# Feed-forward input tiles in pairs of d_ff halves, difference halves made early, scores and values at later slots, ninth chunks of two batches per transfer

## The chip, the cores and the metric

The program runs on one core of one Trainium2 chip. The metric is the device time of one execution in microseconds. The kernel before was run three times: 289.43 us is the median, 286.65 and 290.04 us the lowest and the highest.

## The reference

The inputs are `q`, `k`, `v` of shape 8 batches x 8 heads x 576 positions x 64, and the two weights `w_in` (512 x 2048) and `w_out` (2048 x 512), all float32. Attention stays inside chunks of 64 positions, so each batch has nine chunks per head:

```python
scores = scale * np.matmul(q_c, k_c.transpose(0, 1, 2, 4, 3))     # chunk by chunk
attn = softmax(scores)
x = attn @ v_c            # -> 4608 tokens x 512 (heads side by side)
h = np.maximum(x @ w_in, 0.0)
out = (h * h) @ w_out     # 4608 x 512
```

## The kernel before

**Tiling.** The 4608 tokens are cut into 18 groups of 256 tokens (four chunks of 64), and two groups make a block of 512 tokens: blocks j = 0 to 8. Sixteen groups ("whole") hold four chunks that follow each other in one batch. A batch has nine chunks, so the ninth chunks of all batches are left over; they make groups 14 and 15 (`rest`, line 47), that is block 7. `chunks` gives the four (batch, position) pairs of a group.

**Stages of a block.** For its two groups: load q and k (lines 99 to 121) and v (`v_pieces`, 145 to 153); cast q and k to bf16 (`C`, `cast_qk`, on ScalarE for groups 8 and up); transpose them by DMA (`TD`, line 267); scores and exponential (`SC`, `scores`: 32 small matmuls per group at line 290 and one Exp at 301); values (`AV`, `values`: 32 matmuls at 317 in two tiles, each of which VectorE evicts with a reciprocal at 324 and a multiplication at 325); a DMA transpose of the result x into xT (`XT`, line 338). Then the feed-forward input stage `ffn_in` and the output stage `ffn_out` of the block.

**`ffn_in(j)`** (line 375) makes 16 tiles of d_ff, `ft` = 0 to 15. Each is four matmuls of 128x512 (line 380) into one of four PSUM banks `ps_ffn`, a Relu on ScalarE into `rl` (391), and a square into `gT[:, ft]`: on VectorE (395), or on ScalarE (393) for the `ft` in `SQUARES_ON_ACT`. In blocks 2 to 8 the order is `FT_ORDER`, 8 to 15 and then 0 to 7.

**`ffn_out(j)`** (line 413) multiplies the 512 x 2048 gT by the 2048 x 512 w_out with seven products of quarters in place of eight (Strassen's scheme in Winograd's form). The quarters of gT are a11, a12 (first 256 tokens, `ft` 0 to 7 and 8 to 15) and a21, a22 (last 256 tokens). Each product is 16 matmuls of 128x256 (line 448), 8 for each of two row tiles. The products follow each other as n = a22(b11+b21); m = a11(b12+b22); n += d5 b22; m += d2 b11; n += d1(b11-b22); m += d6(b11+b12); n += d7(b21+b22), in two PSUM banks called n and m. Between them a bank is read out: n1 and n2 by ScalarE copies (492, 501), `nm` (496) and the outputs c21, c12, c22 (508, 517, 522) by VectorE additions, and c11 by a ScalarE copy (528). The next product into a bank waits for that reading. The differences d5 = a11-a12, d2 = a22-a21, d1 = a11-a22, d6, d7 are made by VectorE at line 408, each one instruction on 128x2048 bf16 elements, all inside `ffn_out`: d5 and d2 at its start, d1 after `nm`, d6 after n2, d7 after c21.

**Order of the work.** It is written out by hand. Every `yield` of `ffn_in` (16, slots 0 to 15) and of `ffn_out` (14, slots 16 to 29, one for each half product) is a slot; the loop at line 610 puts the attention of the next block (`nxt`), and the casts and transposes of the block after that (`far`), behind chosen slots of block j. Engines take their instructions in the order in which they stand. In the kernel before, the slots are (lines 642 to 661): scores of both groups at 5, 6, 7 or 8, by block; values at 8 and 12, 9 and 13, or 10 and 14; XT three slots behind each; C at 18 and 22; TD at 20 and 24. Block 2 has its own: scores 8 and 10, values 12 and 15.

**SyncE's queue** issues all loads and all DMA transposes of these blocks. `go_slots` says behind which slots one load each is put: every slot from 0 on, but in block 3 slots 0 to 5 and 13 to 31. A load waits for no other engine here, so it is issued as soon as the queue reaches it and one of eight DMA semaphores is free (each DMA waits for the one that stands eight places before it to have landed). A whole group has 3 loads of q and k and 4 or 5 of v; a `rest` group has 8 and 8, since each chunk is from another batch (`runs`, line 89). Outputs are issued from GpSimd's queue (lines 471 and 476).

Of the kernel before, what the change touches and what calls it, by code (L numbers as in the profile page):

```python
# [10 lines left out]
FP32 = mybir.dt.float32  # L11
# [6 lines left out]
def kernel(  # L18
# [22 lines left out]
    blocks = [[g, g + 1] for g in range(0, n_grp, 2)]  # L41


    CH = GT // 4
    n_ch = S // CH
    whole = [[(b, CH * (4 * i + c)) for c in range(4)] for b in range(B) for i in range(2)]
    rest = [[(b, CH * (n_ch - 1)) for b in range(b0, b0 + 4)] for b0 in range(0, B, 4)]
    chunks = whole[:-2] + rest + whole[-2:]

    def is_whole(g):  # L50
# [27 lines left out]
    NV = 5  # L78
    NO = 2 * NV + 1
    v_even = [w_pool.tile([128, 2, n_hp, D + 1], FP32, name=f"ve_sb{i}") for i in range(NV)]  # L80
    v_odd = [w_pool.tile([128, n_hp, D + 1], FP32, name=f"vo_sb{i}") for i in range(NO)]
    for vt in v_even:
        nc.gpsimd.memset(vt[:, :, :, D:D + 1], 1.0)
    for vt in v_odd:
        nc.gpsimd.memset(vt[:, :, D:D + 1], 1.0)

    qk = {}

    def runs(g):

        for t in range(2):
            (b, s), (b1, s1) = chunks[g][2 * t:2 * t + 2]
            if b == b1:
                yield t, 0, 2 * CH, b, s
            else:
                yield t, 0, CH, b, s
                yield t, CH, CH, b1, s1

    def qk_pieces(g):
        q_sb = in_pool.tile([128, 2, H, D], FP32, name="q_sb")  # L100
        k_sb = in_pool.tile([128, 2, H, D], FP32, name="k_sb")
        qk[g] = (q_sb, k_sb)

        def pairs(dst, src, p, m, b, s):
            return lambda: nc.sync.dma_start(
                out=dst.rearrange("p t h d -> p (t h d)")[p:p + m // 2, :].rearrange(
                    "p (h e) -> p h e", h=H),
                in_=src[b, :, s:s + m, :].rearrange("h (s i) d -> s h (i d)", i=2))

        if is_whole(g):  # L110
            yield pairs(q_sb, q, 0, GT, *chunks[g][0])
        else:
            for c in range(4):
                yield pairs(q_sb, q, c * CH // 2, CH, *chunks[g][c])
        if g < FIRST_DMA_T:
            yield pairs(k_sb, k, 0, GT, *chunks[g][0])
            return
        for t, p, m, b, s in runs(g):
            yield lambda t=t, p=p, m=m, b=b, s=s: nc.sync.dma_start(
                out=k_sb[p:p + m, t, :, :],  # L120
                in_=k[b, :, s:s + m, :].rearrange("h s d -> s h d"))

# [2 lines left out]
    for g in range(n_grp):  # L127
        if is_whole(g):
            if g % 2 == 0:
                first = n_odd  # L130
                n_odd += 5
            b, s = chunks[g][0]
            for c in range(4):
                odd_tile[g, c] = first + g % 2 * 2 + (c + 1) // 2
            odd_loads[g] = [(first, CH, CH, b, s), (first + 1, 0, 2 * CH, b, s + CH),
                            (first + 2, 0, 2 * CH, b, s + 3 * CH)] if g % 2 == 0 else [
                                (first + 3, 0, 2 * CH, b, s + CH), (first + 4, 0, CH, b, s + 3 * CH)]
        else:
            for c in range(4):
                odd_tile[g, c] = n_odd + c // 2  # L140
            odd_loads[g] = [(n_odd + c // 2, (1 - c % 2) * CH, CH, b, s)
                            for c, (b, s) in enumerate(chunks[g])]
            n_odd += 2

    def v_pieces(g):
        for t, p, m, b, s in runs(g):
            yield lambda t=t, p=p, m=m, b=b, s=s: nc.sync.dma_start(
                out=v_even[g % NV][p:p + m, t, :, 0:D],
                in_=v[b, 0::2, s:s + m, :].rearrange("h s d -> s h d"))
        for n, p, m, b, s in odd_loads[g]:  # L150
            yield lambda n=n, p=p, m=m, b=b, s=s: nc.sync.dma_start(
                out=v_odd[n % NO][p:p + m, :, 0:D],
                in_=v[b, 1::2, s:s + m, :].rearrange("h s d -> s h d"))

    def go(pieces):
# [147 lines left out]
    def values(g, tiles=(0, 1)):  # L303
        e = state["e", g]
        veb = v_even[g % NV].bitcast(BF16)
        vob = [v_odd[odd_tile[g, c] % NO].bitcast(BF16) for c in range(4)]
        if 0 in tiles:
            state["x", g] = att_pool.tile([128, 2, n_hp, 2, D], BF16, name="x", bufs=3)
        x = state["x", g]
# [58 lines left out]
            transpose_x_early(g, t)  # L368

    gTs = {}  # L370
    FT_ORDER = [*range(n_ft // 2, n_ft), *range(n_ft // 2)]

    def ffn_in(j, parts):
        if j not in gTs:
            gTs[j] = ffn_pool.tile([128, n_ft, BT], BF16, name="gT")
        gT, xT = gTs[j], xTs[j]
        for u, (c, n, ft) in enumerate((c, n, ft) for c, n, fts in parts for ft in fts):
            h = ps_ffn.tile([128, 512], FP32, name="ps_ffn")
            for dt in range(n_dt):
                nc.tensor.matmul(  # L380
                    out=h[:, 0:n],
                    lhsT=w_in_bf[:, dt, ft * 128:(ft + 1) * 128],
                    rhs=xT[:, c // 128:(c + n) // 128, dt, :],
                    start=(dt == 0), stop=(dt == n_dt - 1))
# [6 lines left out]
            nc.scalar.activation(out=rl[:, 0:n], in_=h[:, 0:n], func=AF.Relu)  # L391
            if (n == 512 and ft in SQUARES_ON_ACT) or (n < 512 and (j == 0 or ft in (12, 3))):
                nc.scalar.activation(out=gT[:, ft, c:c + n], in_=rl[:, 0:n], func=AF.Square)  # L393
            else:
                nc.vector.tensor_tensor(  # L395
                    out=gT[:, ft, c:c + n], in0=rl[:, 0:n], in1=rl[:, 0:n], op=ALU.mult)
            yield

    HF, HD = n_ft // 2, d_model // 2
    b11, b12 = w_out_bf[:, 0:HF, 0:HD], w_out_bf[:, 0:HF, HD:]
    b21, b22 = w_out_bf[:, HF:, 0:HD], w_out_bf[:, HF:, HD:]
    b11_p_b21, b11_m_b22, b11_p_b12 = (w_sum[:, i] for i in range(3))
# [8 lines left out]
    def ffn_out(j):  # L413
# [2 lines left out]

        gT = gTs.pop(j)
        HT = BT // 2  # L420
        last = j == len(blocks) - 1
        a11, a12 = gT[:, 0:HF, 0:HT], gT[:, HF:, 0:HT]
        a21, a22 = gT[:, 0:HF, HT:], gT[:, HF:, HT:]

        def difference(x, y):
            d = wst_pool.tile([128, 1024], FP32, name="w_st").bitcast(BF16).rearrange(
                "p (a f) -> p a f", a=HF)
            add(nc.vector, d, x, y, ALU.subtract)
            return d
# [34 lines left out]
        def store(dma, o_sb, half, col, t):  # L464
# [3 lines left out]
            if not is_whole(g):  # L468

                for p in range(2):  # L470
                    dma.dma_start(
                        out=out.rearrange("(b s) d -> s b d", s=S)[
                            s0:s0 + CH, b + p:b + 4:2, col:col + HD],
                        in_=o_sb[p * CH:(p + 1) * CH].rearrange("p (t d) -> p t d", d=HD))
            elif t is None:
                dma.dma_start(  # L476
# [7 lines left out]
        def o_tile():  # L484
            return ffn_pool.tile([128, n_tt * HD], FP32, name="o_sb", bufs=4)

        d5 = difference(a11, a12)
        d2 = difference(a22, a21)
        yield from product("n", a22, b11_p_b21, True)
        n1 = kept("n1")  # L490
        for ps, cols, t in parts("n"):
# [2 lines left out]
        w = kept("nm")  # L494
        for ps, cols, t in parts("m"):
            add(nc.vector, w[:, cols], ps, n1[:, cols])
        d1 = difference(a11, a22)
        yield from product("n", d5, b22, False)
        n2 = kept("n2")
        for ps, cols, t in parts("n"):  # L500
            nc.scalar.copy(out=n2[:, cols], in_=ps)  # L501
        d6 = difference(a21, a11)
        if j == 1:
            d7 = difference(a12, a22)
        yield from product("m", d2, b11, False)
        c21 = o_tile()
        for ps, cols, t in parts("m"):
            add(nc.vector, c21[:, cols], w[:, cols], ps, ALU.subtract)
            store(nc.gpsimd, c21, 1, 0, t)
        if j > 1:  # L510
            d7 = difference(a12, a22)
        yield from product("n", d1, b11_m_b22, False)
        s = kept("n1")
        for ps, cols, t in parts("n"):
# [50 lines left out]
            yield from v_pieces(g)  # L565


    HT = BT // 2
    first_ffn_in = ffn_in(0, [(0, HT, (0, 1)), (HT, HT, (0, 1)), (0, BT, range(2, n_ft))])

    go(pieces([0, 1]))
# [38 lines left out]
    for j, grps in enumerate(blocks):  # L610
# [29 lines left out]
            at(20, sum_quarters(b21_p_b22, b21, b22), None)  # L640
            phases = [ffn_in(1, [(0, 256, FT_ORDER), (256, 256, FT_ORDER)]), ffn_out(1)]
        else:
            loads, go_slots = pieces(far), range(32)
            slots = {SC: (6, 6), AV: (9, 13), XT: (12, 16), C: (18, 22), TD: (20, 24)}
            if j == 3:
                slots.update({SC: (8, 8), AV: (10, 14), XT: (13, 17)})
                go_slots = [*range(6), *range(13, 32)]
            elif j == 4:
                slots.update({SC: (7, 7), AV: (10, 14), XT: (13, 17)})
            elif nxt and is_whole(nxt[0]):  # L650
                slots.update({SC: (5, 5), AV: (8, 12), XT: (11, 15)})
# [7 lines left out]
            for f in (C, TD):  # L659
                for i, g in enumerate(far):  # L660
                    at(slots[f][i], f, g)
            phases = [ffn_in(j, [(0, BT, FT_ORDER)]), ffn_out(j)]
        slot = 0
        for phase in phases:
            for _ in phase:
# [39 lines left out]
```

## Time and profile before

| what | value |
|---|---|
| median of three runs | 289.43 us |
| the profiled execution | 286.88 us |
| its span, first to last instruction | 285.1 us |
| granted TensorE clock | 1.00 |
| busy: TensorE matmuls | 270.0 us |
| busy: VectorE, ScalarE, GpSimd | 186.4, 163.3, 57.6 us |
| all DMA traffic | 57.10 MB, mean 200 GB/s |
| first matmul of the input stage of blocks 2 to 8 | 82.90, 111.04, 139.16, 167.75, 195.83, 225.78, 255.10 us |

The profile is that of one execution. Times in it are microseconds from the start of the span. A row of the timeline gives the start, the length, the engine (DVE is VectorE, ACT ScalarE, PE TensorE, SP SyncE), the line of the kernel, what is written from what is read, the number of instructions, and in brackets the idle time before it and what ended that. A row of groups ends with busy time, the mean duration of one in ns, and the idle time before it. The length of a row counts from the start of its first instruction to the end of its last; engines begin the next instruction before the last one's result is out, so the steps between starts are shorter than the durations (matmuls of 128x512: 379 ns each, a step of 216 ns).

### The profile page before, as it was taken

The page shows a single profiled execution, that of the slowest core. Times are in us where ns is not written, and L with a number is a line of the kernel's source. Part 1 is how long each engine was busy: PE and PEld are TensorE (multiplying, and loading weights), DVE is VectorE, ACT ScalarE, POOL GpSimd, SP SyncE. Part 2 cuts the span into 40 slices and gives each one's busy share as a digit, 9 for nine tenths or more (in the row PEclk, how much of TensorE's full clock was granted, in tenths as well). Part 3 has the DMA queues.
Part 4 walks back from the last instruction along what each step waited for, and adds up shares of the span by engine and source line. Part 5 has one row for each costly group of instructions (what it writes and reads, how often), then busy time and mean ns, then how long its engine had stood idle before and what let it go on. Part 6 is the DMA issues. An engine that isn't in the chain of part 4 may idle for free. (4 is left out here: it accounts for less than half of the span.)

```text
span 285.1 us, 7166 instructions
## 1 busy us (share of the span) xinstructions
PE 270.0 (95%) x2951; PEld 175.5 (62%) x2954; DVE 186.4 (65%) x303; ACT 163.3 (57%) x277; POOL 57.6 (20%) x92
## 2 busy tenths in 40 slices
PE   2999999999999999999999999999799989999994
PEld 1554454788774587458645864586358734874583
DVE  1254614898943695589549954995389538965792
ACT  1557705786358762966396639663866287218710
POOL 2028935153171004000300030003000400050012
PEclk9999999999999999999999999999999999999999
DMA  7999999999999999999999899599999962132003
GB/s 204 236 298 322 380 351 223 328 225 213 213 232 259 229 215 247 261 233 170 256 219 215 176 260 245 107 134 196 212 221 184 257 113 39 37 96 55 1 24 125
DMA packets 140817, 57.10 MB, mean 200 GB/s; under 512 B 110640, under 2 KB 137520, under 8 KB 140784
## 3 DMA queue, kind: packets, MB, share of 16 engines
q1 hardware_dynamic: 137744, 47.33, 76.2%
q0 software_dynamic: 2896, 9.18, 9.7%
q8 instruction: 23, 0.38, 0.6%
q10 hardware_dynamic: 144, 0.13, 0.1%
q14 instruction: 10, 0.08, 0.1%
HBM read 36.70 MB, written 9.44 MB: 162 GB/s over the span
## 5 line engine op out<-in xcount | busy, mean ns | idle before, releaser
L380 PE MATMUL ps_ffn<-xT,w_in_bf 128*128 128x512 bf16 (+1 forms) x648 | 130.5, 356 | 0.9 <-POOL w_in_bf L169 0.3
L395 DVE TENSOR_TENSOR gT<-rl 128x512 bf16<-128x512 f32 (+2 forms) x130 | 73.6, 593 | 65.4 <-ACT rl L391 63.6
L391 ACT ACTIVATE rl<-ps_ffn 128x512 f32<-128x512 f32 (+2 forms) x162 | 86.0, 548 | 27.3 <-PE ps_ffn L380 24.4
L380 PEld LDWEIGHTS <-w_in_bf 128*128 128x128 bf16 x648 | 61.2, 98 | 58.0 <-POOL w_in_bf L169 1.0
L448 PEld LDWEIGHTS <-w_st 128*128 128x128 bf16 x640 | 61.7, 98 | 8.8 <-DVE w_st L408 1.4
L408 DVE TENSOR_TENSOR w_st<-gT 128x2048 bf16<-128x2048 bf16 x40 | 47.3, 1219 | 0.2
L448 PE MATMUL ps_ffn<-w_out_bf,w_st 128*128 128x256 bf16 x384 | 45.1, 273 | 0.3
L476 POOL DMA_DIRECT2D out_dram<-o_sb x25 | 17.8, 714 | 128.3 <-DVE o_sb L408 123.7
L448 PE MATMUL ps_ffn<-w_sum,w_st 128*128 128x256 bf16 x256 | 29.6, 273 | 0.0
L448 PEld LDWEIGHTS <-gT 128*128 128x128 bf16 x256 | 24.7, 98 | 4.6 <-DVE gT L395 0.3
L325 DVE TENSOR_TENSOR x<-ps_att,rec 128x512 bf16<-128x512 f32 x36 | 24.9, 691 | 1.2
L528 ACT COPY o_sb<-ps_ffn 128x512 f32<-128x512 f32 (+1 forms) x8 | 4.5, 560 | 35.4 <-PE ps_ffn L448 35.4
L301 ACT ACTIVATE e<-ps_att 128x1024 bf16<-128x1024 f32 x18 | 18.0, 1021 | 6.7 <-PE ps_att L290 6.7
L393 ACT ACTIVATE gT<-rl 128x512 bf16<-128x512 f32 (+2 forms) x32 | 18.4, 576 | 1.0
L448 PE MATMUL ps_ffn<-w_out_bf,gT 128*128 128x256 bf16 x128 | 15.4, 273 | 0.0
L448 PE MATMUL ps_ffn<-w_sum,gT 128*128 128x256 bf16 x128 | 15.3, 273 | 0.0
L538 PE MATMUL ps_ffn<-w_out_bf,gT 128*128 128x512 bf16 x61 | 14.2, 379 | 0.3 <-issue 0.2
L169 POOL CAST w_in_bf<-w_st 128x512 bf16<-128x512 f32 (+2 forms) x12 | 9.6, 816 | 19.2 <-DMA w_st<-in_moe_w_in_dram 18.9
L290 PEld LDWEIGHTS <-qkT 64*64 64x64 bf16 x576 | 6.2, 110 | 9.4 <-issue 3.6
L501 ACT COPY n<-ps_ffn 128x512 f32<-128x512 f32 (+1 forms) x9 | 4.8, 539 | 11.9 <-PE ps_ffn L448 11.9
L290 PE MATMUL ps_att<-qkT 64*64 64x64 bf16 x576 | 8.3, 198 | 3.4 <-DMA qkT<-qkb 3.0
L317 PEld LDWEIGHTS <-e 64*64 64x64 bf16 x576 | 6.5, 107 | 7.4 <-issue 2.2
(53 smaller groups left out, 167.7 us busy)
## 6 DMA issues: line engine op xcount, KB each, us to landing
q_sb<-in_q_dram SPq DMA_DIRECT2D x16, 512.0 KB, 6.4
out_dram<-o_sb POOLq DMA_DIRECT2D x29, 256.0 KB, 4.6
k_sb<-in_k_dram SPq DMA_DIRECT2D x24, 256.0 KB, 5.9
ve_sb<-in_v_dram SPq DMA_DIRECT2D x32, 128.0 KB, 4.2
w_st<-in_moe_w_in_dram SPq DMA_DIRECT2D x8, 512.0 KB, 6.3
w_st<-in_moe_w_out_dram SPq DMA_DIRECT2D x8, 512.0 KB, 5.8
vo_sb<-in_v_dram SPq DMA_DIRECT2D x24, 128.0 KB, 3.8
k_sb<-in_k_dram SPq DMA_DIRECT2D x4, 512.0 KB, 6.7
```

What stands on the lines that cost most here:

```text
L169: copy(out=dst, in_=st[:, rows].rearrange("p a (f t) -> p a t f", t=2)[:, :, t])
L290: nc.tensor.matmul(out=ps[64 * c:64 * c + 64, o0:o0 + 64], lhsT=qkT[64 * a:64 * a + 64, 1, t, hp, cols], rhs=queries(a, t, hp, p), start=T ...
L301: nc.scalar.activation(out=e_out, in_=s_in, func=AF.Exp, scale=scale)
L325: nc.vector.tensor_tensor(out=x[:, t].rearrange("p h a d -> p a h d"), in0=o[:, :, :, 0:D], in1=rec.to_broadcast([128, 2, n_hp, D]), op=AL ...
L380: nc.tensor.matmul(out=h[:, 0:n], lhsT=w_in_bf[:, dt, ft * 128:(ft + 1) * 128], rhs=xT[:, c // 128:(c + n) // 128, dt, :], start=(dt == 0) ...
L391: nc.scalar.activation(out=rl[:, 0:n], in_=h[:, 0:n], func=AF.Relu)
L393: nc.scalar.activation(out=gT[:, ft, c:c + n], in_=rl[:, 0:n], func=AF.Square)
L395: nc.vector.tensor_tensor(out=gT[:, ft, c:c + n], in0=rl[:, 0:n], in1=rl[:, 0:n], op=ALU.mult)
L408: engine.tensor_tensor(out=out, in0=in0, in1=in1, op=op)
L448: nc.tensor.matmul(out=outs[t], lhsT=a[:, i, t * 128:(t + 1) * 128], rhs=b[:, i, :], start=(first and i == 0 and (last or t == 0)), stop=( ...
L476: dma.dma_start(out=out[t0:t0 + HT, col:col + HD].rearrange("(t p) d -> p t d", p=128), in_=o_sb.rearrange("p (t d) -> p t d", d=HD))
L538: nc.tensor.matmul(out=o_ps[tt], lhsT=gT[:, ft, tt * 128:(tt + 1) * 128], rhs=w_out_bf[:, ft, :], start=(ft == 0), stop=(ft == n_ft - 1))
```

## The change

- `rest` pairs batches b and b+4 within a tile, so that two neighbouring batches' ninth chunks lie in one half of the partitions. k and v of a `rest` group come with one transfer for two batches: 2 loads of k in place of 4, 4 of v in place of 8. The stores of block 7 follow the new order (line 471).
- The eleven tiles `v_odd` become one tile with eleven places, filled with ones by one memset in place of eleven.
- In blocks 2 to 8 the tiles of `ffn_in` come as pairs, `ft` = 8, 0, 9, 1, ..., 15, 7. ScalarE squares four of them (0, 10, 3, 4), in place of three (10, 14, 3).
- Half of d5 (`ft` 0 to 3 and 8 to 11) is made in `ffn_in` behind the tenth tile (u = 9), half of d2 behind u = 11, half of d1 behind u = 13. `ffn_out` makes the other halves where it made the whole.
- In blocks 3 to 7 scores of both groups stand at slot 11, values at 14 and 18, XT at 17 and 21; the last two fall into `ffn_out`. C and TD stay at 18, 22 and 20, 24. Loads stand at slots 0 to 5 (0 to 11 when the groups to load are `rest` groups) and from 13 on. Block 2 keeps its slots.

```diff
-    rest = [[(b, CH * (n_ch - 1)) for b in range(b0, b0 + 4)] for b0 in range(0, B, 4)]
+    rest = [[(b0 + t + p * (B // 2), CH * (n_ch - 1)) for t in range(2) for p in range(2)]
+            for b0 in range(0, B // 2, 2)]
...
     SQUARES_ON_ACT = (10, 14, 3)
+    SQUARES_ON_ACT_PAIRS = (0, 10, 3, 4)
...
-    v_odd = [w_pool.tile([128, n_hp, D + 1], FP32, name=f"vo_sb{i}") for i in range(NO)]
+    v_odd = w_pool.tile([128, NO, n_hp, D + 1], FP32, name="vo_sb")
...
-    for vt in v_odd:
-        nc.gpsimd.memset(vt[:, :, D:D + 1], 1.0)
+    nc.gpsimd.memset(v_odd[:, :, :, D:D + 1], 1.0)
...
+        if not is_whole(g):
+            for p in range(2):
+                b, s = chunks[g][p]
+                yield lambda p=p, b=b, s=s: nc.sync.dma_start(
+                    out=k_sb[p * CH:(p + 1) * CH].rearrange("p t h d -> p (t h) d"),
+                    in_=k.rearrange("b h s d -> s (b h) d")[s:s + CH, b * H:(b + 2) * H])
+            return
...
+    HF, HD, HT = n_ft // 2, d_model // 2, BT // 2
+    DIFFERENCES = {"d1": (0, 3), "d2": (3, 2), "d5": (0, 1), "d6": (2, 0), "d7": (1, 3)}
+    EARLY_DIFFERENCES = {9: "d5", 11: "d2", 13: "d1"}
+
+    def quarters(j):
+
+        return [gTs[j][:, a:a + HF, c:c + HT] for c in (0, HT) for a in (0, HF)]
+
+    def difference(j, name, part):
+        if (name, j) not in state:
+            state[name, j] = wst_pool.tile([128, 1024], FP32, name="w_st").bitcast(BF16).rearrange(
+                "p (a f) -> p a f", a=HF)
+        x, y = (quarters(j)[i][:, part] for i in DIFFERENCES[name])
+        nc.vector.tensor_tensor(out=state[name, j][:, part], in0=x, in1=y, op=ALU.subtract)
     FT_ORDER = [*range(n_ft // 2, n_ft), *range(n_ft // 2)]
+
+    FT_PAIRS = [ft + h for ft in range(n_ft // 2) for h in (n_ft // 2, 0)]
...
+            on_act = SQUARES_ON_ACT_PAIRS if fts is FT_PAIRS else SQUARES_ON_ACT
+            if (n == 512 and ft in on_act) or (n < 512 and (j == 0 or ft in (12, 3))):
...
+            if n == BT and fts is FT_PAIRS and u in EARLY_DIFFERENCES:
+                difference(j, EARLY_DIFFERENCES[u], slice(0, HF // 2))
             yield
...
+        def rest_of(name):
+            difference(j, name, slice(HF // 2 if (name, j) in state else 0, HF))
+            return state[name, j]
...
-        d5 = difference(a11, a12)
-        d2 = difference(a22, a21)
+        d5 = rest_of("d5")
+        d2 = rest_of("d2")
         yield from product("n", a22, b11_p_b21, True)
...
-            loads, go_slots = pieces(far), range(32)
-            slots = {SC: (6, 6), AV: (9, 13), XT: (12, 16), C: (18, 22), TD: (20, 24)}
-            if j == 3:
-                slots.update({SC: (8, 8), AV: (10, 14), XT: (13, 17)})
-                go_slots = [*range(6), *range(13, 32)]
-            elif j == 4:
-                slots.update({SC: (7, 7), AV: (10, 14), XT: (13, 17)})
-            elif nxt and is_whole(nxt[0]):
-                slots.update({SC: (5, 5), AV: (8, 12), XT: (11, 15)})
+            loads, n_qk = pieces(far), 6 if not far or is_whole(far[0]) else 12
+            go_slots = [*range(n_qk), *range(13, 32)]
+            slots = {SC: (11, 11), AV: (14, 18), XT: (17, 21), C: (18, 22), TD: (20, 24)}
...
-            phases = [ffn_in(j, [(0, BT, FT_ORDER)]), ffn_out(j)]
+            phases = [ffn_in(j, [(0, BT, FT_PAIRS)]), ffn_out(j)]
```

More of the change, by code (lines that the diff above doesn't have):

```diff
@@ L80 @@
     v_even = [w_pool.tile([128, 2, n_hp, D + 1], FP32, name=f"ve_sb{i}") for i in range(NV)]
-    v_odd = [w_pool.tile([128, n_hp, D + 1], FP32, name=f"vo_sb{i}") for i in range(NO)]
+    v_odd = w_pool.tile([128, NO, n_hp, D + 1], FP32, name="vo_sb")
     for vt in v_even:
         nc.gpsimd.memset(vt[:, :, :, D:D + 1], 1.0)
-    for vt in v_odd:
-        nc.gpsimd.memset(vt[:, :, D:D + 1], 1.0)
+    nc.gpsimd.memset(v_odd[:, :, :, D:D + 1], 1.0)
     qk = {}
[L89 to L97, printed above, removed]
     def qk_pieces(g):
@@ L117, in qk_pieces @@
             return
[L118 to L121, printed above, removed]
+        if not is_whole(g):
[5 more added lines that the diff above has]
+            return
+        for t in range(2):
+            b, s = chunks[g][2 * t]
+            yield lambda t=t, b=b, s=s: nc.sync.dma_start(
+                out=k_sb[:, t, :, :],
+                in_=k[b, :, s:s + 2 * CH, :].rearrange("h s d -> s h d"))
     odd_tile, odd_loads = {}, {}
@@ L138 @@
         else:
+            assert n_odd % NO < NO - 1
             for c in range(4):
                 odd_tile[g, c] = n_odd + c // 2
-            odd_loads[g] = [(n_odd + c // 2, (1 - c % 2) * CH, CH, b, s)
-                            for c, (b, s) in enumerate(chunks[g])]
             n_odd += 2
     def v_pieces(g):
[L146 to L149, printed above, removed]
+        if not is_whole(g):
+            n = odd_tile[g, 0] % NO
+            for a, dst in ((0, v_even[g % NV]), (1, v_odd[:, n:n + 2])):
+                for p in range(2):
+                    b, s = chunks[g][p ^ a]
+                    yield lambda a=a, p=p, b=b, s=s, dst=dst: nc.sync.dma_start(
+                        out=dst[p * CH:(p + 1) * CH].rearrange("p t h d -> p (t h) d")[:, :, 0:D],
+                        in_=v.rearrange("b (h a) s d -> a s (b h) d", a=2)[
+                            a, s:s + CH, b * n_hp:(b + 2) * n_hp])
+            return
+        for t in range(2):
+            b, s = chunks[g][2 * t]
+            yield lambda t=t, b=b, s=s: nc.sync.dma_start(
+                out=v_even[g % NV][:, t, :, 0:D],
+                in_=v[b, 0::2, s:s + 2 * CH, :].rearrange("h s d -> s h d"))
         for n, p, m, b, s in odd_loads[g]:
             yield lambda n=n, p=p, m=m, b=b, s=s: nc.sync.dma_start(
-                out=v_odd[n % NO][p:p + m, :, 0:D],
+                out=v_odd[p:p + m, n % NO, :, 0:D],
                 in_=v[b, 1::2, s:s + m, :].rearrange("h s d -> s h d"))
@@ L305, in values @@
         veb = v_even[g % NV].bitcast(BF16)
-        vob = [v_odd[odd_tile[g, c] % NO].bitcast(BF16) for c in range(4)]
+        vob = [v_odd[:, odd_tile[g, c] % NO].bitcast(BF16) for c in range(4)]
         if 0 in tiles:
@@ L376, in ffn_in @@
         gT, xT = gTs[j], xTs[j]
-        for u, (c, n, ft) in enumerate((c, n, ft) for c, n, fts in parts for ft in fts):
+        for u, (c, n, fts, ft) in enumerate((*p, ft) for p in parts for ft in p[2]):
             h = ps_ffn.tile([128, 512], FP32, name="ps_ffn")
@@ L391, in ffn_in @@
             nc.scalar.activation(out=rl[:, 0:n], in_=h[:, 0:n], func=AF.Relu)
-            if (n == 512 and ft in SQUARES_ON_ACT) or (n < 512 and (j == 0 or ft in (12, 3))):
+            on_act = SQUARES_ON_ACT_PAIRS if fts is FT_PAIRS else SQUARES_ON_ACT
+            if (n == 512 and ft in on_act) or (n < 512 and (j == 0 or ft in (12, 3))):
                 nc.scalar.activation(out=gT[:, ft, c:c + n], in_=rl[:, 0:n], func=AF.Square)
@@ L396, in ffn_in @@
                     out=gT[:, ft, c:c + n], in0=rl[:, 0:n], in1=rl[:, 0:n], op=ALU.mult)
+            if n == BT and fts is FT_PAIRS and u in EARLY_DIFFERENCES:
+                difference(j, EARLY_DIFFERENCES[u], slice(0, HF // 2))
             yield
-    HF, HD = n_ft // 2, d_model // 2
     b11, b12 = w_out_bf[:, 0:HF, 0:HD], w_out_bf[:, 0:HF, HD:]
@@ L413, in ffn_out @@
     def ffn_out(j):
-        gT = gTs.pop(j)
-        HT = BT // 2
         last = j == len(blocks) - 1
[L422 to L429, printed above, removed]
+        a11, a12, a21, a22 = quarters(j)
+        def rest_of(name):
+            difference(j, name, slice(HF // 2 if (name, j) in state else 0, HF))
+            return state[name, j]
         n_tt = HT // 128
@@ L472, in store @@
                         out=out.rearrange("(b s) d -> s b d", s=S)[
-                            s0:s0 + CH, b + p:b + 4:2, col:col + HD],
+                            s0:s0 + CH, b + p * (B // 2):b + p * (B // 2) + 2, col:col + HD],
                         in_=o_sb[p * CH:(p + 1) * CH].rearrange("p (t d) -> p t d", d=HD))
@@ L496, in ffn_out @@
             add(nc.vector, w[:, cols], ps, n1[:, cols])
-        d1 = difference(a11, a22)
+        d1 = rest_of("d1")
         yield from product("n", d5, b22, False)
@@ L501, in ffn_out @@
             nc.scalar.copy(out=n2[:, cols], in_=ps)
-        d6 = difference(a21, a11)
+        d6 = rest_of("d6")
         if j == 1:
-            d7 = difference(a12, a22)
+            d7 = rest_of("d7")
         yield from product("m", d2, b11, False)
@@ L510, in ffn_out @@
         if j > 1:
-            d7 = difference(a12, a22)
+            d7 = rest_of("d7")
         yield from product("n", d1, b11_m_b22, False)
@@ L565, in pieces @@
             yield from v_pieces(g)
-    HT = BT // 2
     first_ffn_in = ffn_in(0, [(0, HT, (0, 1)), (HT, HT, (0, 1)), (0, BT, range(2, n_ft))])
```

## Prediction

> **What bounds the kernel now.** I read busy time by stage first, cut at the first input-stage matmul of blocks 3 to 8.
>
> ```profile
> 111.04:139.16 28.12, 28.02 (x306) 18.06 (x304) 20.52 (x31) 18.15 (x28) 2.85 (x5) 1.00 1.05 231
> 139.16:167.75 28.59, 28.20 (x306) 18.19 (x304) 20.63 (x31) 18.16 (x28) 2.85 (x5) 1.00 1.06 222
> 167.75:195.83 28.08, 27.98 (x306) 18.07 (x304) 20.44 (x31) 18.30 (x28) 2.86 (x5) 1.00 0.88 184
> 195.83:225.78 29.95, 28.17 (x307) 18.28 (x305) 20.62 (x31) 18.71 (x29) 3.01 (x5) 1.00 1.06 203
> 225.78:255.10 29.32, 28.15 (x305) 18.35 (x305) 20.43 (x31) 14.44 (x24) 3.67 (x6) 1.00 0.39 87
> 255.10:281.60 26.50, 26.04 (x177) 17.03 (x174) 18.37 (x28) 13.44 (x25) 4.80 (x9) 1.00 0.17 51
> ```
>
> After the window come its length, then the busy time of TensorE, its weight loads, VectorE, ScalarE and GpSimd. TensorE is busy nearly throughout: it is the bound, and only its gaps can be won. Blocks 3 to 7 take 144.06 us together. The timeline and the waits of TensorE say where the longer blocks lose:
>
> ```profile
> 203.97 0.45 PE L290 MATMUL ps_att<-qkT 64*64 64x64 bf16 x32 [1.55 <-DMA qkT<-qkb]
> 225.78 5.34 PE L380 MATMUL ps_ffn<-xT,w_in_bf 128*128 128x512 bf16 x24 [0.22 <-DMA xT<-x]
> 232.66 0.45 PE L290 MATMUL ps_att<-qkT 64*64 64x64 bf16 x32 [1.17 <-DMA qkT<-qkb]
> ```
>
> ```profile
> PE ps_att L290 <- DMA qkT<-qkb: 3.0, 3, 1.6
> ```
>
> Scores at slots 5 to 7 come before their transposed q and k. Last I read block 3's stage boundary on VectorE and ScalarE:
>
> ```profile
> 127.81 0.69 DVE L325 TENSOR_TENSOR x<-ps_att,rec 128x512 bf16<-128x512 f32 x1
> 128.42 0.68 DVE L395 TENSOR_TENSOR gT<-rl 128x512 bf16<-128x512 f32 x1
> 129.14 2.36 DVE L408 TENSOR_TENSOR w_st<-gT 128x2048 bf16<-128x2048 bf16 x2
> 131.41 0.69 DVE L408 TENSOR_TENSOR nm<-ps_ffn,n 128x512 f32<-128x512 f32 x1
> ```
>
> ```profile
> 118.45 1.16 ACT L391 ACTIVATE rl<-ps_ffn 128x512 f32<-128x512 f32 x2
> 119.50 1.93 ACT L301 ACTIVATE e<-ps_att 128x1024 bf16<-128x1024 f32 x2
> 121.31 1.10 ACT L391 ACTIVATE rl<-ps_ffn 128x512 f32<-128x512 f32 x2
> ```
>
> TensorE enters the output stage at 126.60, but VectorE ends the last square at 129.10 and d5 at 130.36. TensorE reads d5 at 130.42, 0.31 late. Block 3 without this is 27.81 us, my floor for blocks 3 to 7. They lose 144.06 - 5 x 27.81 = 5.0 us: the most that can come back.
>
> **What the Trainium skill says.** "TensorE: Matmul & The Clock Gate", Specifications: ScalarE and VectorE queues are strict FIFO. The trace agrees: block 3's d5 (129.14) stands behind eviction and last square. "DMA: Bandwidth & Descriptors", Anatomy of one DMA: engines of the DMA don't wait on semaphores, the issuing sequencer does. The trace agrees: SyncE held a transpose of q and k from 135.30 to 139.14, and issued the load behind it at 139.23.
>
> **Price of a half difference.** The trace has only whole ones, with a step of 1.135 us (two in 2.27). A bf16 square of 512 elements steps by 0.353 (three in 1.06, block 2), so 1024 elements interpolate to 0.61. "VectorE: DVE Perf Modes", The TRN2 errata, gives 58 + elements/2 cycles at 0.96 GHz: 1.127 for the whole, near the 1.135, and 0.594 for the half. I take 0.61 (both ends, 0.59 and 0.61, are alike). Other steps from this trace: float32 square 0.605; the eviction of a group's values 1.69 (123.17 to 124.86); Relu 0.55, result after 0.60, start 0.20 after the matmul; Exp 0.905 (two in 1.81); on TensorE a tile 0.865, a group's scores 0.36, its values 0.50, a half product 0.874. From a VectorE result to TensorE 0.06.
>
> **Edits off the path.** Eleven memsets of 106 ns become one: GpSimd saves about 1 us in the first 4.92 us, when TensorE waits for q; nothing, and without that cover still under 1 us. Twelve of 32 loads go for groups 14 and 15, each 0.6 us of SyncE's queue: 7 us of queue, hidden under TensorE except where it made qkT late (203.93), which the later scores also cure. A fourth ScalarE square adds 0.545 us to ScalarE, idle 10 us a block, and saves VectorE 0.605; it falls before u = 10. Three split differences cost VectorE 3 x (2 x 0.61 - 1.135) = 0.26 us a block, counted below. `v_odd` in one tile: by the program's order each load waits for readers of its own place, two blocks back: nothing.
>
> **Scores at slot 11.** The last transpose of q and k ends its issue near T + 13 (T: end of the input stage) and lands by T + 17; the next block starts near T + 13.95 and reaches slot 11 after 12 tiles, at T + 24. The qkT waits go.
>
> **The boundary in blocks 3 to 7.** The built order puts on VectorE, behind slot 11: squares of u = 12 and 13, half d1, square u = 14 (`ft` 15), eviction of the first group, square u = 15 (`ft` 7), rest of d5, rest of d2, eviction of the second group, `nm`. Time 0 is TensorE's end of tile u = 11.
>
> TensorE: scores to 0.72, tiles to 3.315, values to 3.815, last tile to T = 4.68. ScalarE: Relu of u = 11 from 0.20 to 0.75, two Exps to 2.56, Relu of u = 12 out at 3.16; the next three at 3.71, 4.26, 4.88. VectorE from 3.19: three squares and half d1, `ft` 15 out at 5.69; eviction to 7.30; `ft` 7 out at 7.99; rest of d5 (which reads it) to 8.64, of d2 to 9.25; eviction to 10.94; `nm` out at 11.62.
>
> Pairing has moved `ft` 15 from u = 7 to u = 14. The first product, which covered the last squares, now needs it in its eighth matmul, at 5.44: TensorE waits 0.31. Product m needs `ft` 7 at 7.50 and gets it at 8.05: 0.55. After the second values (0.50), d5 is in time, but m += d2 b11 waits for `nm`: due 11.29, released 11.68: 0.39. Together 1.25 us a block in place of block 3's 0.31. d1, d6, d7 follow in time (c21 ends about 14.1, d7 15.2, read at 16.9). What SyncE's new order does is the first rival.
>
> **Blocks 2 and 8.** Block 2 keeps its slots and gets the pairs; squares are 0.353. From the end of u = 12: d2's half to 1.69, square to 2.05, eviction 3.74, square, half d1, `ft` 15 out at 5.13. TensorE has passed values, three tiles and values by 3.60 and needs it 0.76 later: 0.83 late, in place of the 0.11 at 102.30. So +0.72. Block 8: half d1 stands before the square of `ft` 15, out at T + 1.0, due T + 0.76: +0.30.
>
> **Sum.** Blocks 3 to 7: 5 x (27.81 + 1.25) - 144.06 = +1.24. With 0.72 and 0.30: +2.3 us. Against the profiled execution (286.88, span 285.1) that is span 287.4, execution 289.2; the median shown is 2.55 above that execution, so 291.7 us there.
>
> **Rivals.** *The second XT comes late.* In SyncE's queue it now stands behind TD of the first group (slot 20), where it stood ahead. x is out near T + 6.3; SyncE, past the first XT (x out at T + 2.8, issued in 1.27) and three loads of 0.6, reaches TD at T + 5.9, issues it in 1.8 us, then one load, then XT (1.27): done T + 9.7, landing 2.0 to 3.4 later, T + 11.7 to 13.1. The next block needs it at T + 13.95. But TD's issue took 3.8 us in block 3 (135.30 to 139.14): then XT lands up to T + 15.1, a wait of 1.1 a block, +5.5 in five: 297.2. Decides: XT landing after T + 13.95. For: 0.22 at 225.78 with an output store beside it. Against: loads pause in this stretch.
>
> *VectorE is not late, and the kernel gets faster.* If squares and halves stay hidden, all 5.0 us come back: 284.4. Decides: a boundary loss below (5.0 - 1.0)/5 = 0.80 us a block gives a gain. For: VectorE is busy only 20.5 of 28 us. Against: it is idle before 3.19, and the loss follows from one queue of measured steps.
>
> *It doesn't do what it says*: qkT still late at slot 11. That needs 7 us more in its landing than above; or gains and losses cancel: 289.4.
>
> **How the numbers follow.** Forecast 0.52, own range 289.5 to 294 (boundary loss 0.8 to 1.6 a block). Late XT 0.20, hidden VectorE 0.20, cancelling 0.08. Range 284.8 to 297.2, which leaves out about a tenth on each side. Two per cent is 283.6 and 295.2 (about what a measurement of this kernel tells from no change): slower has 0.15 of the late XT and 0.04 of the forecast's tail, faster a third of the hidden case, 0.06.
>
> **What would show it.** Right: no TensorE wait on qkT from block 4 on; waits on squares in the first two quarter products and on `nm` before d2 b11, 1 to 1.5 us a block; blocks 4 to 7 all near 29.1 us. Wrong: blocks near 27.8 (Exps earlier, or steps shorter), or waits on xT at block starts.

## The result and the profile after

| kernel | median | lowest to highest | ratio to before, 95% interval |
|---|---|---|---|
| before, six runs | 287.77 us | 284.15 to 290.04 | |
| changed, six runs | 302.63 us | 300.92 to 304.13 | 1.062 [1.055, 1.069] |

The change makes the kernel 6% slower, above the whole predicted range. The profiled execution of the changed kernel took 302.61 us (span 300.7), 15.7 us more than that of before. Ratios here and below are of undisturbed runs alone, medians of all runs, so the two can differ where a kernel's runs spread; the traces of e5, e7, e9, e11 and e13 are of slower runs.

The same cut by stage, at the first input-stage matmul of blocks 2 to 8, shows where the time went (window, length, busy time of TensorE, weight loads, VectorE, ScalarE and GpSimd, granted clock, share of the transfer engines, GB/s):

```profile
82.80:113.77 30.97, 28.51 (x307) 18.33 (x304) 17.29 (x33) 19.54 (x30) 6.66 (x9) 1.00 1.10 214
113.77:149.28 35.51, 28.47 (x304) 18.20 (x305) 20.21 (x33) 18.52 (x30) 3.58 (x5) 0.97 1.02 226
149.28:180.65 31.37, 30.61 (x305) 18.67 (x304) 20.30 (x33) 18.15 (x29) 2.14 (x3) 0.93 0.87 158
180.65:211.93 31.28, 28.45 (x304) 18.17 (x304) 20.21 (x33) 18.96 (x30) 3.57 (x5) 1.00 1.15 195
211.93:241.16 29.23, 28.45 (x304) 18.07 (x303) 20.22 (x33) 17.97 (x29) 2.13 (x3) 1.00 0.91 190
241.16:270.11 28.95, 28.30 (x304) 18.20 (x305) 20.21 (x33) 14.58 (x25) 3.58 (x6) 1.00 0.32 73
270.11:296.72 26.61, 26.38 (x178) 17.03 (x175) 17.37 (x29) 13.82 (x26) 4.90 (x9) 1.00 0.16 46
```

The loss sits in blocks 2 to 5; blocks 6 and 7 are near the 29.06 us of the forecast (27.81 + 1.25). Next to last in each row stands the transfer engines' share: in blocks 2 to 6 it is 0.87 to 1.15 (over 1 where packets overlap), in block 7 a third. The waits of TensorE name what was late (us in total, times, longest):

```profile
PE ps_ffn L407 <- DMA xT<-x: 9.1, 3, 6.4
...
PE ps_ffn L472 <- DVE gT L423: 2.0, 6, 0.4
PE ps_att L301 <- DMA qkT<-qkb: 1.9, 2, 1.6
PE ps_ffn L472 <- DVE nm L437: 1.0, 5, 0.2
```

gT and `nm` are the boundary loss of the forecast. The first line is the rival's: the second XT of the next block comes late. In the timeline, 6.40 us of its 9.1 stand at the start of block 4:

```profile
113.77 10.53 PE L407 MATMUL ps_ffn<-xT,w_in_bf 128*128 128x512 bf16 x48 [0.56 <-DMA xT<-x]
...
149.28 12.68 PE L407 MATMUL ps_ffn<-xT,w_in_bf 128*128 128x512 bf16 x48 [6.40 <-DMA xT<-x]
```

The same 48 matmuls take 2.15 us longer behind that gap: the trace has the granted clock at 0.5 for 6.83 us from 146.85. SyncE's queue between block 3's input stage (its end, T, is at 128.84) and block 4's start:

```profile
131.01 2.16 SPq L158 DMA_DIRECT2D ve_sb<-in_v_dram  x2
133.21 2.83 SPq L162 DMA_DIRECT2D vo_sb<-in_v_dram  x3
136.15 1.26 SPq L349 DMA_TRANSPOSE xT<-x  x1
137.46 1.21 SPq L158 DMA_DIRECT2D ve_sb<-in_v_dram  x2
138.77 0.45 SPq L162 DMA_DIRECT2D vo_sb<-in_v_dram  x1
139.31 3.96 SPq L278 DMA_TRANSPOSE qkT<-qkb  x1
143.37 1.07 SPq L162 DMA_DIRECT2D vo_sb<-in_v_dram  x1
144.54 1.89 SPq L349 DMA_TRANSPOSE xT<-x  x1
```

The first XT, whose x was out before 132, is issued at 136.15, behind loads of v that should have been gone; then comes TD with 3.96 us, then the second XT, which lands at 149.24, T + 20.4. The queue was already late in block 2, whose slots the change leaves alone: its second TD ended its issue at 91.46, in the kernel before at 87.21. That delay is not in the forecast, nor in the first rival as priced. The changed kernel, and then before:

```profile
82.52 8.93 SPq L278 DMA_TRANSPOSE qkT<-qkb  x2
```

```profile
79.70 7.51 SPq L267 DMA_TRANSPOSE qkT<-qkb  x2
```

### The profile page after: what moved, and what is told of

Read it like the earlier page. It is cut to its first block, busy times and chain, and to the rows that moved or that the text cites. A ratio compares the mean times of both kernels' runs of the same rounds, so it can differ in the third digit from the quotient of the medians.

```text
span 300.7 us, 7156 instructions
## 1 busy us (share of the span) xinstructions
PE 274.1 (91%) x2954; PEld 175.6 (58%) x2954; DVE 183.9 (61%) x317; ACT 165.4 (55%) x284; POOL 55.8 (19%) x82
## 5 line engine op out<-in xcount | busy, mean ns | idle before, releaser
L423 DVE TENSOR_TENSOR gT<-rl 128x512 bf16<-128x512 f32 (+2 forms) x123 | 69.4, 592 | 79.4 <-ACT rl L418 78.9
L407 PEld LDWEIGHTS <-w_in_bf 128*128 128x128 bf16 x648 | 62.1, 99 | 70.5 <-issue 12.4
L418 ACT ACTIVATE rl<-ps_ffn 128x512 f32<-128x512 f32 (+2 forms) x162 | 84.5, 548 | 33.2 <-PE ps_ffn L407 32.3
L395 DVE TENSOR_TENSOR w_st<-gT 128x1024 bf16<-128x1024 bf16 (+1 forms) x61 | 50.5, 851 | 0.2
L421 ACT ACTIVATE gT<-rl 128x512 bf16<-128x512 f32 (+2 forms) x39 | 22.9, 586 | 1.2
L472 PE MATMUL ps_ffn<-w_out_bf,gT 128*128 128x256 bf16 x128 | 17.0, 273 | 1.8 <-DVE gT L423 1.8
L472 PE MATMUL ps_ffn<-w_sum,gT 128*128 128x256 bf16 x128 | 16.3, 273 | 0.6 <-DVE gT L423 0.2
L525 ACT COPY n<-ps_ffn 128x512 f32<-128x512 f32 (+1 forms) x9 | 4.8, 537 | 14.9 <-PE ps_ffn L472 14.9
L272 ACT CAST qkb<-k_sb 128x1024 bf16<-128x1024 f32 x10 | 10.5, 1047 | 2.0 <-DMA k_sb<-in_k_dram 2.0
L516 ACT COPY n<-ps_ffn 128x512 f32<-128x512 f32 (+1 forms) x9 | 4.8, 538 | 11.0 <-PE ps_ffn L472 11.0
```

The lines of the kernel that those rows point to most:

```text
L272: copy(out=qkb[:, 1], in_=k_sb)
L395: nc.vector.tensor_tensor(out=state[name, j][:, part], in0=x, in1=y, op=ALU.subtract)
L407: nc.tensor.matmul(out=h[:, 0:n], lhsT=w_in_bf[:, dt, ft * 128:(ft + 1) * 128], rhs=xT[:, c // 128:(c + n) // 128, dt, :], start=(dt == 0) ...
L423: nc.vector.tensor_tensor(out=gT[:, ft, c:c + n], in0=rl[:, 0:n], in1=rl[:, 0:n], op=ALU.mult)
L472: nc.tensor.matmul(out=outs[t], lhsT=a[:, i, t * 128:(t + 1) * 128], rhs=b[:, i, :], start=(first and i == 0 and (last or t == 0)), stop=( ...
```

## The experiments

Run beside them, the kernel before had medians of 286.6 to 288.6 us. Numbers of SyncE's landings and of tile addresses are from the trace and the built program.

**Taking the change apart.** First, the order of XT and TD alone, the new slots without pairs, the pairs without the new slots, and the merged loads alone.

```diff
-            slots = {SC: (11, 11), AV: (14, 18), XT: (17, 21), C: (18, 22), TD: (20, 24)}
+            slots = {SC: (11, 11), AV: (14, 18), XT: (17, 21), C: (18, 22), TD: (22, 25)}
```

> The changed kernel with TD at slots 22 and 25, so that both transposes of x stand ahead of both transposes of q and k in SyncE's queue; nothing else changes. Theory A (the second transpose of x is late because of its place, and the long wait also halves TensorE's clock for a while): the 9.1 us of waits on xT and the 2.2 us that block 4 loses at half clock go, and 302.6 becomes about 291. Theory B (SyncE's queue is behind with its loads, whatever stands in it): the waits on xT stay, 299 or more. Theory C (the loss is the stage boundary on VectorE): 300 or more.

293.58 us, ratio 1.030 [1.022, 1.038]. Blocks 4 to 7 now take 28.93 to 28.95 us each, about the floor of 27.81 and the forecast's boundary loss; what is left over is in blocks 2 (31.44) and 3 (30.41).

```diff
-            phases = [ffn_in(j, [(0, BT, FT_PAIRS)]), ffn_out(j)]
+            phases = [ffn_in(j, [(0, BT, FT_ORDER)]), ffn_out(j)]
```

> The changed kernel with the old order of input tiles (8 to 15, then 0 to 7), three squares on ScalarE, and whole differences in the output stage; the new slots and the merged transfers stay. Theory A: the place of the transposes is the same, so the waits on xT stay: 300 to 304 (the boundary in blocks 3 to 7 would then cost some 1.7 us in place of 1.25, by the same steps). Theory C: the pairs were the loss, about 290.

302.94 us, 1.059 [1.050, 1.067]. Blocks 5 to 7 take 30.05 us. TensorE's waits on `nm` grow from 1.0 to 6.3 us, those on the squares from 2.0 to 3.3:

```profile
PE ps_ffn L407 <- DMA xT<-x: 7.4, 2, 6.6
PE ps_ffn L472 <- DVE nm L437: 6.3, 5, 1.3
...
PE ps_ffn L472 <- DVE gT L423: 3.3, 5, 0.7
```

So with the late slots the pairs and early halves save 1.1 us a block; the longest wait on the late XT is much the same without them.

```diff
-            go_slots = [*range(n_qk), *range(13, 32)]
-            slots = {SC: (11, 11), AV: (14, 18), XT: (17, 21), C: (18, 22), TD: (20, 24)}
+            slots = {SC: (6, 6), AV: (9, 13), XT: (12, 16), C: (18, 22), TD: (20, 24)}
...
```

> The changed kernel with the slots and load slots of the kernel before; pairs, early halves of differences and merged transfers stay. Theory A: no waits on xT, and with scores at 5 to 8 and values at 8 to 14 the queue of VectorE is clear at the boundary: 286 to 289, the kernel before within 1 us. Theory C: 295 or more.

300.31 us, 1.051 [1.042, 1.059]: my expectation missed. Waits on gT are 12.2 us in eight, up to 2.8: with values at 12 to 14 the second group's eviction and half d1 stand on VectorE ahead of the square of `ft` 15. This run also has the shift of tiles that the next one (e4) brings to light; against e4, which has the same slots and the same places of tiles but no pairs, the pairs cost 6.3 us. Pairs need the late slots as much as the late slots need pairs.

The fourth keeps before's slots and order and has only the merged loads and the one tile `v_odd`:

> The kernel before with only the merged transfers of the ninth chunks, the new pairing of batches and one tile for the odd heads' v. Theory A: the wait of 1.55 us on q and k of group 15 goes, nothing else: 286 to 288 where the kernel before has 287.8. Rival D (the one tile or the merging is what delays block 2, whose start to end grew by 2.8 us in the changed kernel, 1.6 of it on q and k of group 7): 290 or more, with block 2 near 31 us.

293.97 us, 1.030 [1.020, 1.040]; blocks 2 and 4 take 30.37 and 32.86 us where before had 28.14 and 28.59. That is too early for the merged loads: the first of them is issued in block 5. Up to there the instructions and their order are before's, but for the memsets. What differs is where the tiles lie: eleven tiles step by 1056 bytes and the single one holds 11 x 1040 = 11,440, rounded up to 11,456. So every tile made after it lies 160 bytes lower in its partition, at 32 modulo 64 bytes where it was at 0.

**The place of the tiles.** An unused tile after `v_odd` moves the later ones and changes no instruction:

```diff
     v_odd = w_pool.tile([128, NO, n_hp, D + 1], FP32, name="vo_sb")
+    w_pool.tile([128, 8], FP32, name="pad")
```

> The changed kernel with one unused 32-byte tile after the odd rows' tile, so that every tile made after it stands at a multiple of 64 bytes in its partition again, as in the kernel before; nothing else differs. If the placing slows the transfers (theory): the 256-byte packets of SyncE's queue return from 23.9 ns to about 22.2 ns, blocks 2 and 3 lose about 2 us each, the second XT comes earlier in blocks 4 to 6 but still behind TD: 292 to 298 us. If placing has no part (rival): 301 to 304 us, packets still at 23.9 ns.

291.92 us (288.89 to 297.54), 1.010 [1.003, 1.018].

> The merged loads and the single tile of odd rows alone (old slots, no pairs), with the same unused 32-byte tile. If the placing is what cost 6 us there: 286 to 288.5 us, blocks 2 and 4 back at 28.1 us. If the merged memset or the merged loads themselves cost it: 292 to 296 us.

283.72 us, 0.990 [0.985, 0.995]: 10 us less than e4 for 32 unused bytes, and less than before.

> The kernel before with one unused 32-byte tile after the eleven tiles of odd rows, so that the later tiles stand at 32 modulo 64 bytes; no instruction differs. If the placing costs time: 291 to 295 us, packets of 256 bytes at 23.5 to 24 ns, waits for qkT at 4 us or more. If it doesn't: 287 us, plus or minus 1.5.

299.72 us (296.23 to 303.36), 1.037 [1.029, 1.046], with these waits in a run of 303.36 us:

```profile
PE ps_att L291 <- DMA qkT<-qkb: 13.5, 6, 5.8
...
PE ps_ffn L381 <- DMA xT<-x: 2.1, 1, 2.1
```

The kernel before, moved by 32 bytes, loses 12 us by its medians. The delay that SyncE's queue had in block 2 belongs to the place of the tiles too: the second TD there ends its issue at 88.9 to 91.5 us in all nine traces of this document in which x and qkb stand at 32 modulo 64 bytes, and at 85.0 to 88.4 in the eleven others. The last of this set has both causes undone:

> The changed kernel with the XT pairs issued ahead of TD (slots 22 and 25 for TD) and the unused 32-byte tile. If the two causes add up (theory: the order of XT and TD, and the placing): 293.6 less the 5.6 us that blocks 2 and 3 had over 28.9, so 288 to 289.5 us, which is the kernel before within 2%. If placing has no part: 293 to 294 us.

288.00 us over 20 runs, 1.004 [1.002, 1.007]. Its waits and its blocks are those of the forecast:

```profile
PE ps_ffn L473 <- DVE gT L424: 2.0, 6, 0.4
PE ps_ffn L473 <- DVE nm L438: 1.0, 5, 0.2
```

```profile
81.30:110.03 28.73, 28.37 (x307) 18.23 (x304) 17.09 (x33) 18.50 (x29) 4.05 (x6) 1.00 0.99 224
110.03:138.96 28.93, 28.29 (x307) 18.17 (x305) 20.20 (x33) 18.46 (x29) 2.85 (x5) 1.00 1.05 217
138.96:167.89 28.93, 28.29 (x307) 18.18 (x305) 20.21 (x33) 18.46 (x29) 2.86 (x5) 1.00 1.02 208
...
254.68:281.29 26.61, 26.38 (x178) 17.06 (x175) 17.36 (x29) 13.82 (x26) 4.90 (x9) 1.00 0.16 45
```

No wait on qkT, none on xT. Its queue between blocks 3 and 4 (the input stage ends at 125.08, block 4 starts at 138.96):

```profile
129.27 1.26 SPq L350 DMA_TRANSPOSE xT<-x  x1
130.59 2.05 SPq L159 DMA_DIRECT2D ve_sb<-in_v_dram  x2
132.74 1.18 SPq L163 DMA_DIRECT2D vo_sb<-in_v_dram  x2
134.01 1.28 SPq L350 DMA_TRANSPOSE xT<-x  x1
135.39 8.11 SPq L279 DMA_TRANSPOSE qkT<-qkb  x2
```

The second XT lands at 137.13, T + 12.05, and two TDs of together 8.11 us stand behind it and harm nobody. The medians make a table of the two causes:

| | tiles moved by 160 bytes | at 0 modulo 128 |
|---|---|---|
| TD ahead of the second XT | 302.6, 1.062 (changed) | 291.9, 1.010 (e5); 294.4, 1.016 (e11) |
| second XT ahead of TD | 293.6, 1.030 (e1) | 288.0, 1.004 (e8) |

Undoing the order saves 9 us in the moved kernel and 4 to 6 in the other; undoing the shift saves 8 to 11 and 5.6. Together they save 14.6 us, less than the 17 to 20 that the two come to when each is undone by itself: part of the loss needs both. Both delay one queue, which would explain that; no run separates it further.

**Is it packet time?** SyncE's 256-byte packets took 22.2 ns each in before, 23.9 in the changed kernel and 21.0 in e6, so I tried whether a placing at 0 modulo 256 (32 elements of padding in before) buys more, and whether merging by itself is neutral (40 elements after the single tile, so that e10's and e11's later tiles have exactly before's addresses).

> The kernel before with one unused tile of 128 bytes after the tiles of odd rows: the tiles that q, k and the weights are loaded into then stand at 0 modulo 256 bytes in their partition, where they stood at 128; no instruction differs. If the 1% by which the merged loads ran faster at that placing came from the placing (theory): 283 to 285 us, the sum of SyncE's packets at 206 us per transfer engine where before had 217. If it came from the merged loads or the single memset (rival): 287.6 us and 217.

288.13 us, 1.005 [1.001, 1.008]. The packets did as expected (204.0 us per transfer engine, from 217.3), the time didn't move: the theory falls. Less packet time does show at the start: block 2 begins at 81.1 to 81.9 us in the four traces at this place (e5, e6, e8, e9), at 82.4 to 83.4 in the sixteen others. In before no gain is left at the end.

> The merged loads and the single tile alone (old slots, no pairs), with 160 bytes unused after that tile, so that every later tile has exactly the address it has in the kernel before. If merging is neutral by itself (theory, and the forecast's 'nothing'): 286.5 to 289 us, packets summing to 217. If merging itself is what gained: 283 to 285 us.

283.87 us, 0.995 [0.992, 0.998], with packets at 216.9: the rival is right by the median. Merging itself gains a little: with twelve fewer issues, qkT comes in time in blocks 6 and 7, which take 28.38 and 28.07 us where before had 29.95 and 29.16. Only block 7 is clearly due to it: e12, e16 and e17 below, which have before's loads, take 28.38 in block 6 too, and 28.72 to 29.18 in block 7. The wait of 1.55 us in block 6 that the prediction started from stands in none of these three. What is left in e10:

```profile
PE ps_att L302 <- DMA qkT<-qkb: 0.4, 1, 0.4
```

> The changed kernel with 160 bytes unused after the single tile, so that every later tile has exactly the address it has in the kernel before: the change without its shift. Between the run at 0 modulo 256 (about 290 us) and the changed kernel (302.6 us): theory says 293 to 297 us, with an XT wait of 3 us or more left in block 3 or 4; a rival, that any placing at a multiple of 64 bytes does equally well, says 290 to 292 us; that the shift didn't matter, 301 or more.

294.35 us (290.53 to 297.59), 1.016 [1.007, 1.025], with xT waits of 5.7 us in three in a run of 297.44 us: the change without its shift, and still with the late XT.

**Which tiles.** Moving one group at a time by 32 bytes in the kernel before, with padding that keeps all other tiles' place modulo 256.

> The kernel before with two unused tiles around the pool that q and k are loaded into, so that only these ten tiles stand at 32 modulo 64 bytes (160 modulo 256) and all other tiles keep their place modulo 256; no instruction differs. If the cost of the shift is in the loads of q and k (theory): 295 to 300 us and mean 256-byte packets at 23.5 ns or more. If it is in the transposing transfers, the weights' staging or the output (rival): 286 to 290 us, packets at 22 ns.

287.86 us, 1.004 [1.000, 1.008]: not the loads of q and k, against my theory.

> The kernel before with only the attention pool moved by 32 bytes: qkT, e, x, rec, xT and qkb stand at 32 modulo 64 bytes, the tiles of q, k, the weights and the second layer keep their place modulo 256; no instruction differs. xT, qkT, x and qkb are all that the transposing transfers read and write. If these carry the cost of the shift (theory, now that moving the tiles of q and k alone cost nothing that can be told): 294 to 300 us with 6 us or more of waits for qkT, and longer issues of the transposes. If they don't (rival: the weights' staging or the output tiles, or only all of them together): 286 to 290 us.

297.69 us (294.19 to 300.66), 1.038 [1.026, 1.050], 11.4 us of qkT waits in a run of 300.66 us. All tiles of the transposing transfers are in this group, and with them e and rec, which no transfer touches.

> The kernel before with only the pool of the second layer moved by 32 bytes: gT, rl, o_sb and the partial sums stand at 32 modulo 64 bytes; no instruction differs. Of these only o_sb is touched by transfers, as their source. Theory: nothing, 286 to 289 us. Rival, that the output transfers or VectorE's and ScalarE's operations on these tiles carry the cost: 292 us or more, with longer means of the squares or of the output transfers.

289.67 us, 1.014 [1.006, 1.022]: a little slower, not settled.

> The kernel before with only the five staging tiles of the weights moved by 32 bytes (VectorE's sums of quarters go through them too); no instruction differs. Theory: nothing, 286 to 289 us. Rival, that the start's weight transfers or the sums in these tiles carry the cost of the shift: 292 us or more, with the loss in the first three blocks or in the 2048-wide sums.

287.24 us, 1.004 [0.998, 1.010]: nothing. Then the tiles that the transposes write against those that they read:

> The kernel before with only qkT and xT, the tiles that the transposing transfers write (and TensorE reads), moved to 32 modulo 64 bytes; all other tiles keep their place modulo 256; no instruction differs. If the writes of the transposes carry the cost of the shift (theory): 294 to 299 us with 8 us or more of waits for qkT. If it is their reads (rival): 286 to 289 us.

287.70 us, 1.001 [0.997, 1.004].

> The kernel before with only qkb and x, the tiles that the transposing transfers read, moved to 32 modulo 64 bytes; all other tiles keep their place modulo 256; no instruction differs. If the writes carry the cost (theory): 286 to 289 us. If the reads do (rival): 294 to 299 us; if each carries a part: 290 to 293 us in both runs.

294.76 us, 1.031 [1.025, 1.038]. It is the tiles that are read, x and qkb. The engines that write them are no slower in the trace: VectorE's evictions into x take 691 ns and ScalarE's casts into qkb 1048 ns, in before as in e18. So it is the transposes' reads; x alone and qkb alone were not tried. Waits of e17 and then of e18:

```profile
PE ps_att L301 <- DMA qkT<-qkb: 1.2, 1, 1.2
```

```profile
PE ps_att L299 <- DMA qkT<-qkb: 5.5, 3, 3.5
...
PE ps_ffn L391 <- DMA xT<-x: 2.1, 1, 2.1
```

The 14 transposes of q and k hold SyncE 41.7 us in before, 39.8 in e17, 51.5 in e18 (37.2 to 44.1 in e12, e14 and e16). In the busiest stretch the same loss is seen as transfer share; the kernel before, and then e18:

```profile
82.00:111.00 29.00, 29.00 (x314) 18.97 (x313) 17.30 (x31) 18.53 (x29) 5.68 (x8) 1.00 1.05 222
111.00:139.00 28.00, 27.90 (x305) 17.95 (x304) 20.52 (x31) 18.15 (x28) 2.73 (x5) 1.00 1.05 231
```

```profile
82.00:111.00 29.00, 27.30 (x297) 17.36 (x295) 16.43 (x30) 19.05 (x29) 5.18 (x7) 1.00 1.13 213
111.00:139.00 28.00, 27.90 (x305) 17.98 (x303) 20.33 (x32) 18.15 (x28) 2.86 (x4) 1.00 1.17 210
```

The share is up by 8 and 11%, bytes per second are down by 4 and 9%.

**The clock.** In the changed kernel, 24 matmuls on the identity where TensorE would stand idle (`keep_busy` counts in quarters of a matmul):

```diff
         go(loads)
+        if j == 3:
+            keep_busy(96)
```

> The changed kernel with 24 matmuls of 512 columns on the identity between blocks 3 and 4 (about 5.2 us, in the place where TensorE waits 6.4 us for the second XT); their result is not used. If the half clock in block 4 comes from that idle (theory): the granted clock stays at 1.0 there, the first 48 matmuls of block 4 take 10.5 us where they took 12.7, and the time falls by about 2 us, to 300 to 301 us. If the half clock has another cause: 302 to 303 us with the half clock still there; if the added matmuls come in the way: 303 us or more.

299.77 us, 1.049 [1.041, 1.056], 2.9 us less than the changed kernel, of which block 4 has 2.0 (29.35 us for 31.37), with the clock at 1.00:

```profile
142.83 5.13 PE L259 MATMUL ps_ffn<-ident 128*128 128x512 bf16 x23
150.30 10.52 PE L407 MATMUL ps_ffn<-xT,w_in_bf 128*128 128x512 bf16 x48 [2.34 <-DMA xT<-x]
```

The half clock is a consequence of the wait. The Trainium skill, "TensorE: Matmul & The Clock Gate", Part 1, says that the clock halves after an idle window of about 3.4 us; the changed kernel's trace agrees (half clock from 3.97 us into the idle of 6.40). But the length of one idle stretch isn't a safe limit: in e18 one of 2.15 us was followed by 3.41 us at half clock, and in e3 one of 2.78 us was not.

## Why the prediction was wrong

**The step that failed first** is "`v_odd` in one tile: by the program's order each load waits for readers of its own place, two blocks back: nothing." I costed the tile by its waits and not by its size. It moves x and qkb to 32 modulo 64 bytes (224 and 96 modulo 256). Moving these two alone, to 160 and 32, costs before 8 us by its medians (e18); moving everything costs it 12 (e7), and restoring the place in the changed kernel gives 8 to 11 back (e11, e5).

**The mis-sized term** is the rival "the second XT comes late": its mechanism is right (e1), its size was not. It gave TD 1.8 to 3.8 us and an XT landing at T + 15.1 at worst, 1.1 us a block. In the changed kernel TD took 3.96, 3.01, 2.97 and 3.46 us after blocks 3 to 6 and the second XT landed at T + 20.4, 14.1, 16.2 and 14.1. What was missing is above all the backlog. Both x came about when they were forecast (T + 2.6 and T + 6.2), but SyncE was not "past the first XT and three loads" at T + 5.9: it was still in loads of v, issued the first XT at T + 7.3 and reached TD at T + 10.5. That is 4.6 of the 5.3 us by which block 3's XT missed the priced worst case; TD's 3.96 us and the landing (2.8 us after the issue) were about as priced. And a long wait halves the clock, which nothing in the prediction counts (about 2 us, e15). "Against: loads pause in this stretch" was no argument, since a pause in issuing leaves the backlog; the windows that the prediction itself quotes have a transfer share of 1.05, 1.06 and 1.06 in blocks 3, 4 and 6 of before, a column that I didn't read.

**The forecast's own steps held** where those two causes are gone, in e8:

| step | forecast | e8 |
|---|---|---|
| waits on qkT from block 4 on | none | none |
| boundary of blocks 3 to 7 over the floor of 27.81 | 1.25 us each | 1.12 (28.93) |
| block 2 | +0.72 | +0.59 (28.73 for 28.14) |
| block 8 | +0.30 | +0.41 (26.61; 26.20 in before and in e10) |
| sum | +2.3 us | +1.75 (144.65 - 143.90, and 0.59 and 0.41) |

The last cut of before's trace stood wrong: the first input-stage matmul of block 8 is at 254.94, not 255.10, and the last matmul ends at 281.14. So blocks 3 to 7 took 143.90 us and block 8 took 26.20; the forecast's +2.3 should have been +2.4. By its blocks e8 meets the forecast, of a kernel that the change isn't. Its total of 1.004 meets it partly by luck, since its block 2 begins 1.6 us sooner than before's, a gain that no step forecast. "VectorE is not late" is refuted by the waits on gT and `nm`, which all kernels with pairs and late slots show. "Hidden under TensorE", said of the shorter queue, was half right: the merged loads gain by themselves about what qkT waited in block 7 (e10).

**What stays open.** Why reads from 32 modulo 64 bytes are slower, inside the transfer engines, no run shows. The Trainium skill, "DMA: Bandwidth & Descriptors", How a descriptor splits into AXI transactions, says that a descriptor not at a multiple of 256 bytes fetches from the boundary below and pays for it. By that alone a read from 128 should be no cheaper than one from 32; but before runs at 1.005 with qkb at 128 and x at 0 (e9), and at 1.031 with qkb at 32 and x at 160 (e18). Here the measurement decides: places at 32 modulo 64 are slow, multiples of 128 are not. Whether 128 is quite as good as 0 is not shown. e6 (qkb at 128, x at 0) and e10 (the other way round) take the same time, but the transposes of q and k hold SyncE 45.0 us in e6 and 37.1 in e10, and e6's faster loads may hide that. 64 was not tried. Nor is it settled why e14 lost 1.4%. That e7's medians lose 4 us more than e18's may be spread: the intervals of their ratios overlap.

## What to carry to other kernels

When tiles are merged or resized, work out where all later tiles land: an edit with no instruction on the path can move the operands of every transfer behind it, and 32 unused bytes are the test. Where the transfer share of a stage is near 1, don't take an issue to be hidden: follow SyncE's queue through the stage, and put the transfer that is needed first ahead of the long one. At the same share (1.02 and 1.05) e8's long transposes harm nobody, behind both XT. The best version found is the merged loads alone at before's slots, with the tiles at 0 modulo 128 bytes (e6, e10: 283.7 and 283.9 us, 0.990 and 0.995 of before). The pairs and late slots on top of it cost 4.3 us (e8 against e6).

## What was not expected of the hardware

- A transposing transfer that reads a tile at 32 modulo 64 bytes is slower; for one that writes such a tile no loss shows (e18 294.8 us, e17 287.7). The Trainium skill, "DMA: Bandwidth & Descriptors", DMA Transpose (X-bar), Constraints, asks for 32-byte alignment: the kernel runs so, but 3% slower than with 0 and 128.
- The issue of one transpose of q and k held SyncE for anything from 1.6 us (e10) to 7.9 us (e7).
- q's, k's and the weights' tiles at 0 instead of 128 modulo 256 cut the mean 512-byte packet from 30.9 to 28.4 ns (e9): block 2 begins 1 us sooner, and nothing of it is left at the end.
